# Random-feature attention ahead of two expert layers: projections in plain floats on half arrays, products of heads in column groups

## The chip, the cores and the metric

The program runs on one core of a Trainium2 chip. The metric is device microseconds of that core from one launch, the median of several runs. The engines are named as the profile names them: PE (matmuls; PEld is its weight loads), ACT, DVE, POOL, and SP, which issues the DMAs.

## The reference

Three layers follow each other. The change touches the first.

```python
def phi(x):                                   # x: q or k, scaled by 64 ** -0.25
    proj = np.einsum('bhsd,md->bhsm', x, omega)
    h = proj - np.sum(x * x, axis=-1, keepdims=True) / 2.0
    h = h - np.max(h, axis=-1, keepdims=True)
    return np.exp(h) / np.sqrt(m)
kv = np.einsum('bhsm,bhsd->bhmd', phi(k), v)
z = np.sum(phi(k), axis=2)
num = np.einsum('bhsm,bhmd->bhsd', phi(q), kv)
den = np.einsum('bhsm,bhm->bhs', phi(q), z)[..., None] + 1e-06
x = num / den                                 # 4 batches, 8 heads, 576 positions, 64 wide, 128 features
...
for e in range(8):                            # P: gates, balanced over 8 rounds
    out += P[:, e:e+1] * (np.maximum(x @ w1[e], 0.0) @ w2[e])
...
h = x @ w_in
return (h * (1.0 / (1.0 + np.exp(-1.702 * h)))) @ w_out
```

All inputs are float32.

## The kernel before, in words

**Order.** Every instruction is first recorded with a planned duration and with the buffers that it reads and writes (`Plan.add`, L62). `Plan.run` (L112) then lists the instructions of all engines with those durations: PE's recorded order stays, the rest goes by the latest time at which somebody needs it. Each engine's queue gets its instructions in that order and runs them in order. So a planned duration that changes (the first argument of `pe`, `act`, `dve`) changes the order on every queue, and instructions that nobody edits move too.

**Attention** (L796) goes through 36 tiles of 128 positions by all 8 heads: for each batch its key tiles, then its query tiles. The last 64 positions of two batches share a tile, the tail. Step s of the loop handles tile s and prepares later ones:

- `load_tile` (L505), 8 steps ahead: q, k, v from DRAM into buffers `b2`, of which there are 20. `squares` (L537), 5 ahead: POOL squares a tile, DVE sums it.
- `project_in` (L555), 4 ahead: PE transposes two heads at a time, ACT copies the result, scaled, as rounded floats (`hi`, L567), and DVE writes what the rounding left (`lo`, L570).
- `features` (L577), 2 ahead: PE multiplies by omega, two heads at once: the 128 rows are two heads of 64, and omega stands in a matrix of 128 x 256 whose other blocks are zero. Each pair takes three matmuls, hi by hi, hi by lo, lo by hi (L588 to L590), twelve a tile. DVE takes the minimum over features (L596).
- `exps` (L604): two small sums on DVE, then eight exponentials on ACT, one a head (L626).
- Key tiles: `kv_step` (L635) multiplies features by values and a column of ones into the PSUM tile `pair`, one head after the other (L641). Query tiles: `transpose_q` (L661) turns the features (PE L670, ACT copy L675), `attend` (L682) multiplies them by the sums (L692), `divide` (L704) divides, `transpose_x` (L728) turns the result (PE L735, ACT L739, DVE L742). The query tails alone multiply in two halves of 64 columns, since the two halves belong to two batches.

All these PSUM results but `pair` go round the six banks 0 to 5 (`ps`, L445).

**Behind it.** Six query tiles make a block of tokens; there are three. `x_operands(j)` (L959) mixes a block's tiles into operands for a fast matrix product (POOL for the first two blocks, ACT casts, L990) and sends them to DRAM. The expert layers then run in visits of a pair of weight chunks by a block: `up_fast` (L1208) with seven products of six matmuls for each of two chunks (L1220), whose results DVE mixes (L1252), ACT casts (L1230) and POOL completes (operands `h`, L407), and `down` (L1351; matmuls L1365). Down products on chunk 0 come ahead of chunk 1's last up product, those on chunk 1 right behind it. The weights of the first expert are prepared during attention: loaded into `raw`, summed (`raw_sum`, L1113) and split (`split`, L1119: ACT casts, L1126, POOL subtracts, into `w1x` and `w2x`), in the order w1 chunk 0, w1 chunk 1, w2 chunk 0, w2 chunk 1, all through the one buffer `raw0`, all on POOL. The first products of the first visit stand among attention's last two steps.

```python
def fn(half):                                 # kv_step, L639
    for h in range(4 * half, 4 * half + 4):
        nc.tensor.matmul(
            PAIR[:, h // 4, (h % 4) * VW : (h % 4) * VW + D + 1], f[r, h, :], vv[r, h, 0 : D + 1],
            start=first and h % 4 == 0, stop=last, skip_group_check=True,
        )
```

## Time and profile before

| | |
|---|---|
| runs | 2039.96, 2043.42, 2046.22 us, median 2043.42 |
| profiled execution, its time / its span | 2040.57 / 2038.8 us |
| busy of the span | PE 1984.5 us (97%), DVE 1466.4, POOL 1257.5, ACT 1080.3 |
| attention | 0 to about 188 us, 9% of the span |
| behind it, 500 to 1000 us | PE busy 495.0 of 500 |
| granted TensorE clock, mean | 0.995 |

Busy time is that of instructions, not of arithmetic: a busy PE is not PE at its peak. Matmuls overlap in the trace, so the distance from one start to the next tells what one takes, and a group's span is read from start to start. Idle time of an engine that nobody waits for costs nothing.

### The profile page before, as it was taken

Reading aid. Unit: us, or ns where it says so; the run is one execution under the profiler, and the core shown is the slowest. Engines: PE = TensorE matmul, PEld = TensorE weight load, DVE = VectorE, ACT = ScalarE, POOL = GpSimd, SP = SyncE. Lnnn points to the kernel's source line nnn. Section 1 sums busy time; section 2 is a strip of 40 time slices with the busy share of each in tenths; the row PEclk is TensorE's granted clock in tenths of the full one; section 3 lists DMA queues with packets and bytes.
Section 4 is the critical chain, followed back from the end, with each engine's and each line's share of the span. In section 5 each row is a group of like instructions: output and inputs, shape, how many; then the busy total and the mean of one; then the engine's idle time right before and its main releaser. Section 6 shows DMA issues by size and latency. Waiting matters only on the chain.

```text
span 2038.8 us, 39158 instructions
## 1 busy us (share of the span) xinstructions
PE 1984.5 (97%) x14211; PEld 1948.2 (96%) x14211; DVE 1466.4 (72%) x3040; ACT 1080.3 (53%) x2537; POOL 1257.5 (62%) x1207
## 2 busy tenths in 40 slices
PE   8999999999999999999999999999999979999999
PEld 8998999999999999999999999999999979999998
DVE  8885468777776777777776777766666786667766
ACT  6877563754445354454445345444534566745654
POOL 3677774757666585766657485665648264747453
PEclk9999999999999999999999999999999999999999
DMA  9647664756666575676566576556546897645653
GB/s 188 163 157 260 229 224 176 283 208 221 256 243 213 214 268 198 232 269 224 199 249 237 195 266 242 214 206 233 202 180 244 252 290 259 257 152 218 227 193 129
DMA packets 246898, 451.97 MB, mean 222 GB/s; under 512 B 73648, under 2 KB 186800, under 8 KB 246704
## 3 DMA queue, kind: packets, MB, share of 16 engines
q1 hardware_dynamic: 246704, 449.47, 62.8%
q8 instruction: 112, 1.84, 0.4%
q14 instruction: 82, 0.67, 0.1%
HBM read 403.26 MB, written 46.14 MB: 220 GB/s over the span
## 4 chain that ended last, share of the span: by engine, by line
PE 81%; DVE 11%; DMA 3%; ACT 3%; issue 1%; POOL 1%; SPq 0%; DVEq 0%; ACTq 0%; POOLq 0%
PE bank L1220 38%; PE bank L1365 37%; DVE h L407 2%; DVE ring L1252 2%; PE pair L641 2%; DVE acc L1398 1%; DVE bank L1241 1%; DVE x2s L1041 1%; ACT h L1230 1%; PE bank L588 1%; DMA sx<-x2s 1%; DMA sx<-acc 1%; PE bank L589 1%; PE pair L692 1%; PE bank L590 1%
## 5 line engine op out<-in xcount | busy, mean ns | idle before, releaser
L1365 PE MATMUL bank<-w2x,h 128*128 128x256 f32 x7560 | 940.1, 281 | 33.4 <-DVE acc L1398 11.8
L1365 PEld LDWEIGHTS bank<-w2x,h 128*128 128x128 f32 x7560 | 917.4, 188 | 48.9 <-DVE acc L1398 16.4
L1220 PE MATMUL bank<-xo,w1x 128*128 128x384 f32 x5040 | 915.9, 336 | 3.7 <-ACT ring L1230 1.6
L1220 PEld LDWEIGHTS bank<-xo,w1x 128*128 128x128 f32 x5040 | 866.7, 188 | 10.2 <-ACT ring L1230 6.3
L407 POOL TENSOR_TENSOR h<-ring,h 128x384 fp32r<-128x384 f32 x382 | 413.4, 1107 | 96.2 <-ACT h L1230 93.7
L1398 DVE SCALAR_TENSOR_TENSOR acc<-bank,sig,acc 128x256 f32<-128x256 f32 x756 | 328.4, 478 | 146.6 <-PE bank L1365 145.7
L407 POOL TENSOR_TENSOR w1x<-raw,w1x 128x768 fp32r<-128x768 f32 (+1 forms) x120 | 181.3, 1520 | 265.2 <-ACT w1x L1126 256.3
L1230 ACT ACTIVATE bank<-bank 128x384 f32<-128x384 f32 x120 | 57.0, 475 | 461.7 <-PE bank L1220 435.8
L1230 ACT ACTIVATE ring<-bank 128x384 f32<-128x384 f32 x480 | 233.2, 491 | 125.6 <-PE bank L1220 116.7
L407 POOL TENSOR_TENSOR raw<-raw 128x256 f32<-128x256 f32 x320 | 240.7, 777 | 83.8 <-DMA raw<-in_moe_w_dram 55.0
L1279 DVE SCALAR_TENSOR_TENSOR h<-bank,h 128x384 fp32r<-128x384 f32 x288 | 159.1, 554 | 161.0 <-ACT ring L1230 146.0
L1230 ACT ACTIVATE h<-ring 128x384 fp32r<-128x384 f32 x480 | 231.1, 527 | 68.3 <-DVE ring L1252 58.1
L407 POOL TENSOR_TENSOR w2x<-raw,w2x 128x768 fp32r<-128x768 f32 (+1 forms) x120 | 180.9, 1515 | 54.9 <-ACT w2x L1126 54.5
L1230 ACT ACTIVATE h<-bank 128x384 fp32r<-128x384 f32 x360 | 175.5, 493 | 71.2 <-DVE bank L1241 45.1
L1252 DVE SCALAR_TENSOR_TENSOR ring<-bank,ring 128x384 f32<-128x384 f32 x384 | 192.6, 547 | 24.8 <-PE bank L1220 23.3
L407 POOL TENSOR_TENSOR ring<-ring 128x384 f32<-128x384 f32 (+1 forms) x106 | 112.2, 1059 | 155.4 <-ACT ring L1230 143.6
L1241 DVE TENSOR_TENSOR bank<-bank,ring 128x384 f32<-128x384 f32 x240 | 133.6, 560 | 32.4 <-PE bank L1220 31.3
L1391 DVE TENSOR_TENSOR acc<-bank,acc 128x256 f32<-128x256 f32 x252 | 95.7, 419 | 64.7 <-PE bank L1365 63.7
L1126 ACT CAST w2x<-raw 128x768 fp32r<-128x768 f32 (+1 forms) x120 | 82.4, 692 | 84.1 <-POOL raw L407 69.1
L407 DVE TENSOR_TENSOR h<-ring,h 128x384 fp32r<-128x384 f32 x98 | 99.6, 1027 | 1.3 <-ACT h L1230 1.0
L1126 ACT CAST w1x<-raw 128x768 fp32r<-128x768 f32 (+1 forms) x120 | 82.4, 693 | 13.5 <-PE bank L1220 11.9
L626 ACT ACTIVATE acc<-bank,acc 128x128 f32<-128x128 f32 x272 | 75.7, 390 | 8.7 <-DVE acc L619 6.5
(134 smaller groups left out, 1457.9 us busy)
## 6 DMA issues: line engine op xcount, KB each, us to landing
xo<-sx SPq DMA_DIRECT2D x420, 768.0 KB, 6.8
raw<-in_moe_w_dram SPq DMA_DIRECT2D x256, 128.0 KB, 4.3
sx<-x2s SPq DMA_DIRECT2D x126, 128.0 KB, 4.1
x2s<-in_moe_w_in_dram SPq DMA_DIRECT2D x16, 512.0 KB, 5.4
x2s<-in_moe_w_out_dram SPq DMA_DIRECT2D x16, 512.0 KB, 9.0
sx<-ring SPq DMA_DIRECT2D x32, 192.0 KB, 1.9
b<-in_k_dram SPq DMA_DIRECT2D x16, 256.0 KB, 4.5
b<-in_v_dram SPq DMA_DIRECT2D x16, 256.0 KB, 4.5
```

What stands on the lines that cost most here:

```text
L407: lambda e: e.tensor_tensor(out=out(), in0=a(), in1=b(), op=op), r, w,
L626: lambda h=h, pv=pv: nc.scalar.activation(f[:, h, :], pv[:, h % 4, :], AF.Exp, bias=nb[:, h : h + 1], scale=-1.0),
L641: nc.tensor.matmul(PAIR[:, h // 4, (h % 4) * VW : (h % 4) * VW + D + 1], f[r, h, :], vv[r, h, 0 : D + 1], start=first and h % 4 == 0, stop ...
L1126: lambda e, a=a, b=b: nc.scalar.copy(T[w, c, 0][:, a:b], r[:, a:b]), raws, [(w, c, g, 0)],
L1220: nc.tensor.matmul(o(b), T["w1", c, a][:, slot, kk], T["xo"][x][:, y, kk], start=start and kk == 0 and n == 0, stop=kk == 1 and n == 2, sk ...
L1230: rec("ACT", act_us(Q), lambda e: nc.scalar.activation(out(), src(), f, **kw), r, w)
L1241: lambda e: e.tensor_tensor(out=out[0](), in0=a[0](), in1=b[0](), op=op), [a[1], b[1]], [out[1]],
L1252: lambda e: e.scalar_tensor_tensor(out=RT(out), in0=o(b), scalar=0.0, in1=RT(c), op0=ALU.max, op1=op),
L1279: lambda e: e.scalar_tensor_tensor(out=g(), in0=src[0](), scalar=0.0, in1=h().bitcast(F32), op0=ALU.max, op1=ALU.subtract),
L1365: nc.tensor.matmul(bank[i][:, u], T["h", c, a, x][:, t * P : (t + 1) * P], T["w2", c, y][:, slot], start=s and m == 0, stop=c == 1 and m = ...
L1391: lambda e, q=q, i=i, u=u: e.tensor_tensor(out=q, in0=bank[i][:, u], in1=q, op=ALU.add),
L1398: lambda e, q=q, i=i, u=u, g=g: e.scalar_tensor_tensor(out=q, in0=bank[i][:, u], scalar=g, in1=q, op0=ALU.mult, op1=ALU.add),
```

## The change

Five things change in attention, and the planned durations with them.

1. `project_in` makes one plain copy `xt` in float32 and no `lo`. omega is kept once, as it is (128 rows: twice 64).
2. `features` multiplies in plain float32, one head at a time on its 64 rows: head pairs alternate between rows 0 to 63, into one bank, and rows 64 to 127, into another. Eight heads, eight matmuls in the code.
3. `kv_step` and `attend` split the 128 columns of every tile into two groups of 64.
4. `features` looks three steps ahead, `project_in` five, `squares` six. Features alternate between banks 0, 1 and 2, 3; all transposes go through banks 4 and 5 by turns. The turned query features have one buffer of their own.
5. Of the buffers `b2`, 13 hold raw tiles, 4 hold `xt` and one the tail of the values.

```diff
-    turn = {"ps": [0, 1, 2, 3, 4, 5], "f4": [0, 1, 2, 3], "small": {}}
+    turn = {"t": [4, 5], "f": [0, 1, 2, 3], "f4": [0, 1, 2, 3], "small": {}}
...
-        hi, kh = slot(NP * P, kind="hl")
-        lo, kl = slot(NP * P, kind="hl")
-        hi, lo = hi.bitcast(F32R), lo.bitcast(F32R)
-        act(0.63, lambda: nc.scalar.activation(hi, pt, AF.Copy, scale=-SCALE), [kp], [kh])
-        dve(
-            0.69,
-            lambda: nc.vector.scalar_tensor_tensor(
-                out=lo, in0=pt, scalar=-SCALE, in1=hi.bitcast(F32), op0=ALU.mult, op1=ALU.subtract
-            ),
-            [kp, kh], [kl],
-        )
-        return (hi, kh), (lo, kl)
+        xt, kt = slot(NP * P, kind="xt")
+        act(0.63, lambda: nc.scalar.activation(xt, pt, AF.Copy, scale=-SCALE), [kp], [kt])
+        return xt, kt
...
-                    nc.tensor.matmul(o, hi[:, u], om_hi, start=True, stop=False)
-                    nc.tensor.matmul(o, hi[:, u], om_lo, start=False, stop=False)
-                    nc.tensor.matmul(o, lo[:, u], om_hi, start=False, stop=True)
-            pe(6 * 0.12, fn, [kh, kl, "om0", "om1"], [kp])
...
+            for i in range(NP):
+                for e in range(2):
+                    r = slice(e * D, (e + 1) * D)
+                    nc.tensor.matmul(
+                        pj[e][0][:, i * M : (i + 1) * M], xt[r, i * P : (i + 1) * P], om[r, :],
+                        start=True, stop=True, skip_group_check=True,
+                    )
+        pe(0.95, fn, [kt, "om"], [k for _, k in pj])
...
+    COLUMNS = [slice(i * P // 2, (i + 1) * P // 2) for i in range(2)]
...
-                nc.tensor.matmul(
-                    PAIR[:, h // 4, (h % 4) * VW : (h % 4) * VW + D + 1], f[r, h, :], vv[r, h, 0 : D + 1],
-                    start=first and h % 4 == 0, stop=last, skip_group_check=True,
-                )
+                for c in COLUMNS:
+                    nc.tensor.matmul(
+                        PAIR[c, h // 4, (h % 4) * VW : (h % 4) * VW + D + 1], f[r, h, c], vv[r, h, 0 : D + 1],
+                        start=first and h % 4 == 0, stop=last, skip_group_check=True,
+                    )
...
-            pe(8 * 0.1115, lambda half=half: fn(half), heads(kf)[4 * half : 4 * half + 4] + [kv], [PAIRS[half]])
+            pe(
+                16 * 0.03 + 0.05, lambda half=half: fn(half),
+                heads(kf)[4 * half : 4 * half + 4] + [kv], [PAIRS[half]],
+            )
...
-        parts = ((slice(0, P), kvs[b]),) if t < NT else tuple(
-            (slice(i * TAIL, (i + 1) * TAIL), kvs[b - 1 + i]) for i in range(2)
-        )
+        parts = [(c, kvs[b if t < NT else b - 1 + i]) for i, c in enumerate(COLUMNS)]
```

The order of PE in one key step, before (a half of `features`, then of `kv_step`; L561 is `project_in`, L588 to L590 the projections, L641 the products):

```order
L561 MATMUL bank_103<-ident,b_90 128x128 x4
L588 MATMUL bank_104<-xo 128x256
L589 MATMUL bank_104<-xo 128x256
L590 MATMUL bank_104<-xo 128x256
L588 MATMUL bank_104<-xo 128x256
L589 MATMUL bank_104<-xo 128x256
L590 MATMUL bank_104<-xo 128x256
L641 MATMUL pair<-b_89,acc_72 128x65 x4
```

and in the changed program (L551 `project_in`, L568 the projections, L624 the products):

```order
L551 MATMUL bank_104<-ident,b_90 128x128 x4
L624 MATMUL pair<-b_87,acc_72 64x65 x16
L568 MATMUL bank_101<-ring,b_94 128x128
L568 MATMUL bank_102<-ring,b_94 128x128
L568 MATMUL bank_101<-ring,b_94 128x128
L568 MATMUL bank_102<-ring,b_94 128x128
L568 MATMUL bank_101<-ring,b_94 128x128
L568 MATMUL bank_102<-ring,b_94 128x128
L568 MATMUL bank_101<-ring,b_94 128x128
L568 MATMUL bank_102<-ring,b_94 128x128
L551 MATMUL bank_103<-ident,b_92 128x128 x4
```

The halves of a tile no longer alternate between projections and products: all of a tile's products stand together, then all of its projections, on two banks by turns.

PE in a query step of the changed program (L654 is `transpose_q`, with the buffers' numbers):

```order
L654 MATMUL bank4_103<-ident_63,acc0_72 128x128 x4
L654 MATMUL bank5_104<-ident_63,acc0_72 128x128 x4
L568 MATMUL bank0_99<-ring_69,b215_95 128x128
L568 MATMUL bank1_100<-ring_69,b215_95 128x128
L568 MATMUL bank0_99<-ring_69,b215_95 128x128
L568 MATMUL bank1_100<-ring_69,b215_95 128x128
L568 MATMUL bank0_99<-ring_69,b215_95 128x128
L568 MATMUL bank1_100<-ring_69,b215_95 128x128
L568 MATMUL bank0_99<-ring_69,b215_95 128x128
L568 MATMUL bank1_100<-ring_69,b215_95 128x128
L551 MATMUL bank4_103<-ident_63,b24_84 128x128 x4
```

All transposes, of queries, of raw tiles and of results, now go through bank 4 and bank 5.

The order of POOL at the first visit, before, from the sums of chunk 1 of the down weights on (`raw0` the sums, `w2x` the splits, `acc1` the third block, names with `h` the operands of the first visit: in `h021` the first digit is the chunk, 0, the second the operand):

```order
L407 TENSOR_TENSOR raw0_67<-raw0_67 128x256 x3
L407 TENSOR_TENSOR w2x_71<-raw0_67,w2x_71 128x768
L407 TENSOR_TENSOR w2x_71<-raw0_67,w2x_71 128x512
L407 TENSOR_TENSOR acc1_73<-x2s_75,acc2_74 128x384
L407 TENSOR_TENSOR w2x_71<-raw0_67,w2x_71 128x512
L407 TENSOR_TENSOR acc1_73<-x2s_75,acc1_73 128x384
L407 TENSOR_TENSOR ring_69<-ring_69 128x384
L407 TENSOR_TENSOR acc1_73<-x2s_75,acc1_73 128x384
L407 TENSOR_TENSOR acc1_73<-acc1_73,acc2_74 128x384 x2
L407 TENSOR_TENSOR acc1_73<-acc1_73,x2s_75 128x384
L407 TENSOR_TENSOR acc1_73<-acc1_73 128x384
L407 TENSOR_TENSOR h021_2087<-ring_69,h020_2086 128x384
```

and now, from the first operand of the visit on:

```order
L402 TENSOR_TENSOR h031_2316<-ring_69,h030_2315 128x384
L402 TENSOR_TENSOR ring_69<-ring_69 128x384
L402 TENSOR_TENSOR raw0_67<-raw0_67 128x256
L402 TENSOR_TENSOR h021_2314<-ring_69,h020_2313 128x384
L402 TENSOR_TENSOR h041_2318<-ring_69,h040_2317 128x384
L402 TENSOR_TENSOR h141_2332<-ring_69,h140_2331 128x384
L402 TENSOR_TENSOR raw0_67<-raw0_67 128x256 x3
L402 TENSOR_TENSOR w2x_71<-raw0_67,w2x_71 128x768
```

The sums and the split of chunk 1 stood ahead of all operands of the visit; they now stand behind h141, an operand of chunk 1 itself.

## Rows read from the trace of the kernel before

**Rows 1.** the page's head.
```profile
span 2038.8 us, 39158 instructions
```

**Rows 2.** timeline of PE, attention's end to the first down products: start us, us, engine, instructions.
```profile
187.40 0.66 PE L735 MATMUL bank<-ident,acc 128*128 128x128 f32 x4 [0.82 <-DVE acc L721]
...
201.04 1.22 PE L1365 MATMUL bank<-w2x,h 128*128 128x256 f32 x9
...
203.14 1.10 PE L1365 MATMUL bank<-w2x,h 128*128 128x256 f32 x8
```

**Rows 3.** windows in us: PE, PEld, DVE, ACT, POOL busy (instructions); clock, DMA share, GB/s.
```profile
20.00:140.00 120.00, 115.22 (x995) 111.18 (x995) 103.89 (x263) 97.28 (x289) 70.25 (x80) 0.99 0.70 173
140.00:188.00 48.00, 45.00 (x398) 43.24 (x397) 28.51 (x72) 37.16 (x105) 32.19 (x34) 1.00 0.53 186
```

**Rows 4.** timeline of PE over a key step; columns as in rows 2.
```profile
20.22 0.61 PE L561 MATMUL bank<-ident,b 128*128 128x128 f32 x4
...
20.58 0.36 PE L588 MATMUL bank<-xo 128*128 128x256 f32 x1
...
21.38 1.00 PE L641 MATMUL pair<-b,acc 128*128 128x65 f32 x8
...
22.19 0.36 PE L588 MATMUL bank<-xo 128*128 128x256 f32 x1
```

**Rows 5.** timeline of PE, half of a query tail.
```profile
96.33 0.69 PE L692 MATMUL pair<-raw,acc 128*64 128x65 f32 x16
96.95 0.66 PE L735 MATMUL bank<-ident,acc 128*128 128x128 f32 x4
```

**Rows 6.** timeline of PE, half of a key tail, on 64 rows.
```profile
32.27 1.10 PE L641 MATMUL pair<-b,ring 64*128 64x65 f32 x8
33.30 0.39 PE L588 MATMUL bank<-xo 128*128 128x256 f32 x1
```

**Rows 7.** groups of DVE by line, 20 to 140 us: count, busy us, mean ns, idle.
```profile
L570 DVE SCALAR_TENSOR_TENSOR xo<-bank,xo 128x512 fp32r<-128x512 f32 x25 | 17.0, 681 | 0.0
```

**Rows 8.** timeline of ACT, a copy of transposes and a tile's exponentials.
```profile
139.74 0.59 ACT L675 COPY acc<-bank 128x512 f32<-128x512 f32 x1
...
142.41 2.18 ACT L626 ACTIVATE acc<-bank,acc 128x128 f32<-128x128 f32 x8
```

**Rows 9.** timeline of PE after a stop; idle us and releaser in brackets.
```profile
103.22 1.08 PE L641 MATMUL pair<-b,acc 128*128 128x65 f32 x8 [2.56 <-POOL acc L541]
...
104.58 1.27 PE L641 MATMUL pair<-b,acc 128*128 128x65 f32 x8
...
108.97 0.36 PE L588 MATMUL bank<-xo 128*128 128x256 f32 x1
```

**Rows 10.** timeline of POOL, the second block's first mixes and chunk 1's splits.
```profile
147.67 1.97 POOL L407 TENSOR_TENSOR ring<-w2x,xo 128x384 f32<-128x384 f32 x2
...
188.46 3.11 POOL L407 TENSOR_TENSOR w2x<-raw,w2x 128x768 fp32r<-128x768 f32 x2
```

**Rows 11.** groups of POOL by line and shape, 147 to 205 us.
```profile
L407 POOL TENSOR_TENSOR ring<-ring,xo 128x384 f32<-128x384 f32 x8 | 7.9, 1004 | 0.1
...
L407 POOL TENSOR_TENSOR ring<-ring 128x384 fp32r<-128x384 f32 x8 | 7.9, 1003 | 3.5 <-ACT ring L990 3.4
...
L407 POOL TENSOR_TENSOR raw<-raw 128x256 f32<-128x256 f32 x4 | 2.8, 731 | 7.7 <-DMA raw<-in_moe_w_dram 7.7
```

**Rows 12.** the page, part 5, groups by line over the span.
```profile
L407 POOL TENSOR_TENSOR h<-ring,h 128x384 fp32r<-128x384 f32 x382 | 413.4, 1107 | 96.2 <-ACT h L1230 93.7
...
L1230 ACT ACTIVATE h<-ring 128x384 fp32r<-128x384 f32 x480 | 231.1, 527 | 68.3 <-DVE ring L1252 58.1
...
L407 POOL TENSOR_TENSOR w2x<-raw,w2x 128x768 fp32r<-128x768 f32 (+1 forms) x120 | 180.9, 1515 | 54.9 <-ACT w2x L1126 54.5
...
L1252 DVE SCALAR_TENSOR_TENSOR ring<-bank,ring 128x384 f32<-128x384 f32 x384 | 192.6, 547 | 24.8 <-PE bank L1220 23.3
```

**Rows 13.** window as in rows 3, behind that stop.
```profile
105.00:108.00 3.00, 3.00 (x18) 3.00 (x17) 1.58 (x4) 2.95 (x10) 3.00 (x4) 0.53 0.66 244
```

More of the change, by code (lines that the diff above doesn't have):

```diff
@@ L343, in tile_performer_sinkhorn_moe @@
     att = opened(att_pool, "att")
[L344 to L345 removed]
+    for i in range(18):
+        slots["b2" if i < 13 else "xt" if i < 17 else "vt"].append((att.tile([P, H * VW], F32, name=f"b2{i}"), ("b2", i)))
+    F4.append(att.tile([P, H, M], F32, name="f4"))
     H_KEYS = [("h", c, o, a) for c in range(2) for o in range(7) for a in range(2)]
@@ L443, in heads, with ps @@
         return [(key, h) for h in range(H)]
-    def ps():
-        i = taken("ps")
+    def ps(what="t"):
+        i = taken(what)
         return bank[i], ("b", i)
@@ L510, in load_tile @@
         w = VW if what == "v" else D
-        x, kx = raw[key] = slot(H * w, H)
+        x, kx = raw[key] = slot(H * w, H, kind="vt" if key[2] == "tail" and what == "v" else "b2")
         if what == "v":
@@ new lines, in project_in, with features, fn @@
+        act(0.63, lambda: nc.scalar.activation(xt, pt, AF.Copy, scale=-SCALE), [kp], [kt])
+        return xt, kt
+    def features(xt, four):
+        (xt, kt), (four, kf) = xt, four
+        pj = [ps("f") for _ in range(2)]
+        def fn():
+            for i in range(NP):
[6 more added lines that the diff above has]
+        pe(0.95, fn, [kt, "om"], [k for _, k in pj])
+        pvs = [(p.rearrange("p (h m) -> p h m", m=M), k) for p, k in pj]
+        for e, (pv, kp) in enumerate(pvs):
@@ L594, in features @@
             dve(
                 0.69,
-                lambda half=half, pv=pv: nc.vector.tensor_reduce(
-                    out=four[:, H + 4 * half : H + 4 * half + 4], in_=pv, op=ALU.min, axis=AX.X
+                lambda e=e, pv=pv: nc.vector.tensor_reduce(
+                    out=four[:, H : 2 * H].rearrange("p (i e) -> p e i", e=2)[:, e], in_=pv, op=ALU.min, axis=AX.X
                 ),
@@ L809, in column @@
             return divmod(PLACE[token_tile(*seq[i][1:])], ST)
[L811 removed]
+        for s in range(-6, n + 3):
             what, b, t = seq[s] if at(s, "kq") else (None, 0, 0)
             if s == n - 2:
[L814 to L843 removed]
+                plan.add("X", 0.0, lambda e: switch(), (), [k for _, k in slots["b2"] + slots["xt"] + slots["vt"]] + heads(("f4", 4)) + H_KEYS)
+            if at(s + 6, "kq"):
+                squares(*seq[s + 6])
+            if s == -6:
+                products_of_zeros(10)
+            if what == "q":
+                ft = transpose_q(feat.pop(s))
+            if s == -1:
+                products_of_zeros(10)
+            if at(s + 3, "kq"):
+                four = sums.pop(seq[s + 3])
+                pvs = features(ins.pop(s + 3), four)
+                w, b2, t2 = seq[s + 3]
                 if w == "k" and t2 == NT:
@@ L848, in attention @@
                     f2 = F4[i], ("f4", i)
-                feat[s + 2] = f2
-            if what == "q":
-                next(tq)
-                yield s - n, 0
-                steps = [attend(ft, b, t)]
-            if steps:
-                next(steps[0])
-            if at(s + 2, "kq"):
+                feat[s + 3] = f2
                 exps(pvs, four, f2)
+            if at(s + 5, "kq"):
+                ins[s + 5] = project_in(*seq[s + 5])
             if at(s - 1, "q"):
                 transpose_x(xs.pop(s - 1), *column(s - 1))
-            for x in steps:
-                take(x, 3)
+            if what == "q":
+                yield s - n, 0
+                attend(ft, b, t)
+            elif what == "k":
+                f = feat.pop(s)
+                last = seq[s + 1][0] == "q"
+                kv_step(b, t, f, t == 0, last and b % 2 == 0)
+                if last and b % 2 == 1:
+                    kv_step(b, NT, ktail.pop(b // 2), False, True)
             yield s - n, 1
```

75 lines of the change are left out of this document (10 added, 65 removed).

## The prediction

> **What bounds the kernel now.** I read the windows first, then the timelines of PE and POOL, then the groups by line. The span is 2038.8 us [rows 1]; the profiled execution took 2040.57 us as a whole, and the median of the three runs, 2043.42 us, stands 2.85 us above it. The change touches attention alone, which ends with PE's last transposes at 187.40 us [rows 2]. From 20 to 140 us PE is busy 115.2 of 120, that is 96%; DVE 103.9, ACT 97.3, POOL 70.3 [rows 3]. So PE sets the pace there, but three engines lie close together: cutting PE's work is worth no more than the way down to the next engine. From 140 to 188 us PE has 45.0 of 48, ACT 37.2 [rows 3].
>
> A key step of PE begins at 20.22 us: transposes to 20.58, six projections to 21.38, four heads' products to 22.19 [rows 4]; then the other six projections and the other four heads. So a tile's twelve projections take 2 x 0.80 = 1.60 us and its eight heads' products 2 x 0.81 = 1.62 us. Each head's product stands as two matmuls in the trace (x8 for four heads), so one takes 0.81 / 8 = 0.101 us.
>
> **The products in two column groups.** One kind of tile works so already, the tails of the queries: a half of sixteen matmuls of 64 columns lies between 96.33 and 96.95 us, 0.62 us with the change of form behind it [rows 5]. The other tiles go from 1.62 to at most 2 x 0.62 = 1.24 us: **0.38 us saved** for each of 36 tiles less the two query tails. A half of a key tail lasted from 32.27 to 33.30 us [rows 6], so a tail, of which there are four, 2.06 us; it comes to 1.24 too, 0.8 us saved.
>
> A matmul of 64 columns thus took 0.62 / 16 = 0.039 us, below the 0.05 that half of 0.101 would be without any overlap. The Trainium skill ("TensorE: Matmul & The Clock Gate", Part 3: Packing small matmuls) holds that weights load beside a running matmul only where the row group differs, which speaks against column groups. By that rule I estimate 0.05 x 16 = 0.8 us a half and no saving on products: PE would keep 100.9 us of the first window where I find 89.8 below, and attention would gain 22.6 us, not 23.4. The measurement decides.
>
> **The projections on 64 rows.** Eight heads are sixteen matmuls of 128 columns, alternately from two halves of the array and into two banks, as the new order of PE shows. No row has two row halves at work at once. Bounds: 0.039 us each, as for column groups, or 0.101 us each if the halves take turns; and the change of form, which on the key tail cost 1.03 - 0.81 = 0.22 us [rows 4, 6]. That makes 0.84 to 1.84 us, against 1.60. I take half of 0.101, since two halves share the work but each still streams all 128 columns, which no column group did: 0.81 + 0.22 = 1.03 us, **0.57 us saved** a tile. The low operand goes too: DVE loses 25 subtractions in the first window, 17.0 us of its 103.9 [rows 7].
>
> **What attention becomes.** In the first window 25 projections, some 23 products and three key tails fall: 25 x 0.57 + 23 x 0.38 + 3 x 0.8 = 25.4, PE 115.2 - 25.4 = 89.8 us. DVE has 103.9 - 17.0 = 86.9. ACT keeps its 97.3 and is now first. With three engines within 11 us of each other, and two banks for transposes where six went round, I give ACT not the 96% that PE had but 93%: 97.3 / 0.93 = 104.6 us, **15.4 us gained**. At 96% it would be 18.6; at 87%, midway to the 81% that ACT has now, 8.2. In the second window PE falls by 11 x 0.57 + 10 x 0.38 + 0.8 to 34.1, and ACT's 37.2 / 0.93 = 40.0: **8.0 us gained** (9.2 and 5.2 at the ends). Together 23.4 us, so the last transposes come at 187.4 - 23.4 = 164.0 us.
>
> The Trainium skill ("TensorEngine Tiling (Array Packing)", PSUM Bottleneck) warns that tiling makes the matmuls faster but not the copies out of PSUM, which then may set the pace. PE alone would give 25.4 + 10.9 = 36.3 us; the windows side with the warning, as ACT's share stands above what PE has left.
>
> Small edits: one copy of omega in place of two masked halves, a prologue longer by a step, 13 buffers of raw tiles where 20 were. I take nothing for them. The prologue moves exponentials ahead, eight in 2.18 us [rows 8], which later steps have behind them; loads still stand eight steps ahead, and DMA had a share of 0.70 [rows 3]. If that cover goes, the price is a stop such as the one before 103.22 us, 2.56 us [rows 9].
>
> **What is late next.** POOL's work is not cut, and stands in another order. The first expert's weights are split by POOL alone, chunk after chunk through one buffer, with the mixes of the second block of tokens (x_operands) among them. Before, POOL took up that block at 147.67 us and reached chunk 1 of the down weights at 188.46 [rows 10]; PE wanted them at 203.14 [rows 2], so nobody waited. Now chunk 1 of w1 comes behind most of the block, then both chunks of w2. From the block's first mix to the first split of w2's chunk 0 POOL has 32 mixes of 1.00 us, 10 sums of 0.73 and 5 splits of 1.52 [rows 11, 12]: 32.1 + 7.3 + 7.6 = 47.0 us, and 3.5 us of waits for ACT as now [rows 11]. The block can begin 15.4 + 8.0 x 7.67 / 48 = 16.7 us earlier, at 131.0; chunk 0 is then there at 181.5. PE reaches the first down products 201.04 - 187.40 = 13.6 us behind the last transposes [rows 2], at 177.6: it **waits 3.9 us**.
>
> Chunk 1 is worse. Its split now stands on POOL behind h141, the rest of an operand that needs PE's last up product, and PE's down products on chunk 1 come right behind that product. So PE stops for a whole chain: three mixes on DVE, 3 x 0.55; a cast on ACT, 0.53; h141, 1.11; three sums, 3 x 0.73; the split, 1.52 [rows 11, 12]: **7.0 us**. The kernel before has no such wait.
>
> Then the clock. After the stop of 2.56 us the granted clock was 0.53 from 105 to 108 us, so mostly the lower level, 1.2 GHz [rows 9, 13]; from 104.58 to 108.97 us PE took 4.39 us for what takes 0.81 + 0.36 + 0.80 + 0.81 = 2.78 at 2.4 GHz [rows 4, 9]. I add **1.6 us** once.
>
> **The sum.** -23.4 + 3.9 + 7.0 + 1.6 = -10.9 us. On the profiled execution that is 2040.57 - 10.9 = 2029.7 us; runs lie up to 2.85 us above such an execution, and I add half of it: **2031.1 us**.
>
> **Rivals.**
> *POOL keeps up.* The sums and the split of chunk 1 are done before PE comes, and the chain lies beside other products. For it: POOL is busy only 70.3 of 120 us [rows 3]. Against it: the order is fixed. All of 23.4 us stays: 2040.57 - 23.4 + 1.4 = 2018.6 us. Chance 0.22.
> *ACT and DVE get in each other's way.* At 87% attention gains 13.4 us. The second block begins 9.1 us earlier, and POOL's chunk 0 is there at 147.67 - 9.1 + 50.5 = 189.1, PE at 187.4 - 13.4 + 13.6 = 187.6: 1.5 us of waiting, then 7.0 and 1.6. That is -3.3 us, 2038.7 us, and within 0.3% of no change (6.1 us, about what a measurement of this kernel can tell). Chance 0.23.
> *The two banks stop PE: slower.* All transposes, four groups in a query step, now go through banks 4 and 5 by turns. A turn holds a bank for 0.36 us of PE, 0.59 of ACT's copy and whatever stands ahead of the copy on ACT [rows 4, 8]. A query step of PE takes about 1.60 + 1.62 + 4 x 0.36 = 4.66 us before; with two turns a bank in each step, the banks set it once a turn is over 2.33 us, when a copy waits over 1.4 us, five of eight exponentials [rows 8]. If it waits for all eight, a turn is 3.13 us and a step 6.26: 18 x 1.6 = 29 us lost, against 18 x 0.65 = 11.7 gained in key steps, with 8.6 of chain and clock: 2068 us. Against it: in ACT's new order most copies stand between exponentials. Chance 0.10.
> *The row halves take turns.* Projections at 1.84 us: PE has 115.2 + 25 x 0.24 - 23 x 0.38 - 2.4 = 110.1 us, at 96% 114.6, so 5.4 us gained, and 3.2 in the second window; POOL is in time then, chain and clock cost 8.6: 2042.0 us. Chance 0.07.
>
> **How the numbers follow.** The sum above has the rest, 0.38, and lies between 2024 and 2037 by itself. From 2017 to 2044 all cases are held but the slow one and the outer ends of others. Faster by over 0.3%, below 2037.3 us: 0.37 of the forecast, 0.21 of the first rival and 0.05 of the second, 0.63. Within 0.3%: 0.26. Slower: 0.11.
>
> **What would show it.** Right: sixteen projections in about 1 us; a half of products in about 0.6; attention's last transposes near 164 us; PE idle some 7 us before the down products on chunk 1, released by POOL's split, and a lower granted clock behind it. Wrong: transposes that wait for ACT's copies in every query step; projections 0.1 us apart; no gap at the first down products; an attention that ends after 175 us.

## The result and the profile after

The changed kernel takes **2025.82 us** (median of 4 runs, 2024.18 to 2028.46); the kernel before, on the same chip, 2044.82 us (4 runs, 2039.96 to 2048.07). The ratio is 0.991, with a 95% interval from 0.9886 to 0.9935: faster by 0.9%. The forecast was 2031.1 us in a range from 2017 to 2044, and faster with a chance of 0.63. The two medians lie 19.0 us apart; beside the later experiments the kernel before had medians of 2041.2 to 2041.6 us and the changed one, run again (e12 below), 2026.07, so some 3.5 us of the 19.0 come from a kernel before that was slower in that measurement than in the later ones.

The page of the changed kernel, against [rows 1]:

```profile
span 2026.7 us, 40550 instructions
PE 1961.8 (97%) x14931; PEld 1910.6 (94%) x14931; DVE 1430.7 (71%) x2994; ACT 1078.1 (53%) x2536; POOL 1263.8 (62%) x1213
```

The span is 12.1 us shorter. Its windows, of which the first answers to [rows 3] (columns: stretch and length; busy us of PE, PEld, DVE, ACT, POOL; granted clock; DMA share; GB/s):

```profile
20.00:140.00 120.00, 109.48 (x1746) 93.48 (x1748) 102.36 (x266) 107.24 (x334) 69.57 (x83) 0.99 0.72 189
140.00:168.00 28.00, 23.67 (x319) 20.38 (x316) 10.69 (x28) 19.65 (x52) 22.52 (x23) 0.94 0.73 248
168.00:188.00 20.00, 15.70 (x94) 13.29 (x92) 9.71 (x20) 12.62 (x28) 18.52 (x20) 1.00 0.86 292
188.00:212.00 24.00, 17.79 (x129) 17.50 (x130) 4.90 (x10) 9.78 (x25) 23.64 (x26) 0.86 0.44 165
```

In the first window PE (91%), ACT (89%) and DVE (85%) stand within 8 us of each other. Behind it POOL fills up: from 188 us it is busy for 23.64 of 24 us, while PE stands still for a quarter of them.

PE's timeline of a key step, against [rows 4] (start, us, engine, line and operation; products L624, projections L568, transposes L551), and of a key tail, against [rows 6]:

```profile
23.39 1.15 PE L624 MATMUL pair<-b,acc 128*64 128x65 f32 x32
24.47 1.16 PE L568 MATMUL bank<-ring,b 64*128 64x128 f32 x16
25.57 0.65 PE L551 MATMUL bank<-ident,b 128*128 128x128 f32 x4
26.15 1.16 PE L624 MATMUL pair<-b,acc 128*64 128x65 f32 x32
...
31.68 1.15 PE L624 MATMUL pair<-b,ring 64*64 64x65 f32 x32
32.76 1.27 PE L654 MATMUL bank<-ident,acc 128*128 128x128 f32 x8
```

From start to start a tile's products take 1.08 us (1.62 before), its projections 1.10 (1.60), a tail's products 1.08 (2.06).

The end of attention and the first visit of the experts, against [rows 2] (L716 are attention's transposes, L1331 the down products, nine on chunk 0 and then 108 on chunk 1):

```profile
167.65 0.60 PE L716 MATMUL bank<-ident,acc 128*128 128x128 f32 x4
...
178.98 5.50 PE L1186 MATMUL bank<-xo,w1x 128*128 128x384 f32 x30 [2.58 <-ACT bank L1196]
184.32 1.22 PE L1331 MATMUL bank<-w2x,h 128*128 128x256 f32 x9
185.37 1.21 PE L1186 MATMUL bank<-xo,w1x 128*128 128x384 f32 x6
192.53 0.58 PE L1331 MATMUL bank<-w2x,h 128*128 128x256 f32 x1 [5.95 <-ACT w2x L1092]
194.79 14.29 PE L1331 MATMUL bank<-w2x,h 128*128 128x256 f32 x107 [1.68 <-POOL w2x L402]
208.91 1.21 PE L1186 MATMUL bank<-xo,w1x 128*128 128x384 f32 x6
209.96 1.22 PE L1331 MATMUL bank<-w2x,h 128*128 128x256 f32 x9
```

Attention ends 19.75 us earlier than before (187.40). Up to the first down products PE then takes 16.67 us, where it took 13.64, with a stop of 2.58 us. In front of chunk 1 it stops for 5.95 and again for 1.68 us. The 0.86 of the granted clock in the last window is a mean over stretches at 1.2 and at 2.4 GHz. The second block's first down products, at 209.96 us, stood at 216.78 in the kernel before: of 19.75 us 6.82 are left there.

What POOL did in the stop (raw sums, L402 `raw`; the operands' rests, `h`; splits, `w2x`):

```profile
178.05 4.30 POOL L402 TENSOR_TENSOR w2x<-raw,w2x 128x768 fp32r<-128x768 f32 x3
...
186.72 0.72 POOL L402 TENSOR_TENSOR raw<-raw 128x256 f32<-128x256 f32 x1 [0.46 <-DMA raw<-in_moe_w_dram]
187.40 3.53 POOL L402 TENSOR_TENSOR h<-ring,h 128x384 fp32r<-128x384 f32 x3
190.89 2.08 POOL L402 TENSOR_TENSOR raw<-raw 128x256 f32<-128x256 f32 x3
192.93 3.04 POOL L402 TENSOR_TENSOR w2x<-raw,w2x 128x768 fp32r<-128x768 f32 x2
```

Chunk 0 is split until 182.35 us; only then may chunk 1 be loaded into the same raw buffer, and it lands at 186.7. Three rests of h stand ahead of the last three sums, and the split begins at 192.93: the chain of the forecast, with a load ahead of the sums that the forecast did not have, and three rests of h where it had one.

### The profile page after: what moved, and what is told of

It is laid out like the page before. It is cut to its first block, busy times and chain, and to the rows that moved or that the text cites. A ratio compares the mean times of both kernels' runs of the same rounds, so it can differ in the third digit from the quotient of the medians.

```text
span 2026.7 us, 40550 instructions
## 1 busy us (share of the span) xinstructions
PE 1961.8 (97%) x14931; PEld 1910.6 (94%) x14931; DVE 1430.7 (71%) x2994; ACT 1078.1 (53%) x2536; POOL 1263.8 (62%) x1213
## 4 chain that ended last, share of the span: by engine, by line
PE 81%; DVE 10%; ACT 3%; DMA 3%; POOL 2%; issue 1%; SPq 0%; DVEq 0%; ACTq 0%; POOLq 0%
PE bank L1186 39%; PE bank L1331 38%; DVE h L402 2%; DVE ring L1218 1%; DVE acc L1364 1%; DMA sx<-x2s 1%; PE bank L568 1%; DVE bank L1207 1%; DVE acc L578 1%; ACT acc L607 1%; DVE acc L538 1%; ACT h L1196 1%; POOL ring L402 1%; DMA xo<-sx 1%; DVE x2s L1007 1%
## 5 line engine op out<-in xcount | busy, mean ns | idle before, releaser
L1331 PE MATMUL bank<-w2x,h 128*128 128x256 f32 x7560 | 943.4, 282 | 35.0 <-DVE acc L1364 9.1
L1331 PEld LDWEIGHTS bank<-w2x,h 128*128 128x128 f32 x7560 | 920.2, 189 | 51.2 <-DVE acc L1364 13.5
L402 POOL TENSOR_TENSOR h<-ring,h 128x384 fp32r<-128x384 f32 x384 | 416.2, 1109 | 94.0 <-ACT h L1196 91.8
L402 POOL TENSOR_TENSOR w1x<-raw,w1x 128x768 fp32r<-128x768 f32 (+1 forms) x120 | 181.6, 1523 | 268.2 <-ACT w1x L1092 259.8
L402 POOL TENSOR_TENSOR raw<-raw 128x256 f32<-128x256 f32 x320 | 238.8, 772 | 76.0 <-DMA raw<-in_moe_w_dram 49.4
L402 POOL TENSOR_TENSOR ring<-ring 128x384 f32<-128x384 f32 (+1 forms) x108 | 113.1, 1049 | 157.0 <-ACT ring L1196 149.8
L402 POOL TENSOR_TENSOR w2x<-raw,w2x 128x768 fp32r<-128x768 f32 (+1 forms) x120 | 182.8, 1532 | 43.7 <-ACT w2x L1092 39.4
L1092 ACT CAST w2x<-raw 128x768 fp32r<-128x768 f32 (+1 forms) x120 | 82.3, 692 | 91.2 <-POOL raw L402 76.2
L402 DVE TENSOR_TENSOR h<-ring,h 128x384 fp32r<-128x384 f32 x96 | 97.9, 1032 | 2.0 <-ACT h L1196 1.7
L1092 ACT CAST w1x<-raw 128x768 fp32r<-128x768 f32 (+1 forms) x120 | 83.3, 698 | 17.7 <-PE bank L1186 16.1
```

The lines of the kernel that those rows point to most:

```text
L402: lambda e: e.tensor_tensor(out=out(), in0=a(), in1=b(), op=op), r, w,
L1092: lambda e, a=a, b=b: nc.scalar.copy(T[w, c, 0][:, a:b], r[:, a:b]), raws, [(w, c, g, 0)],
L1331: nc.tensor.matmul(bank[i][:, u], T["h", c, a, x][:, t * P : (t + 1) * P], T["w2", c, y][:, slot], start=s and m == 0, stop=c == 1 and m = ...
```

## The experiments

Each ratio is against runs of the kernel before that were taken beside it (median 2044.82 us beside the changed kernel, 2041.2 to 2041.6 us beside the experiments). "Ninth" and "last" are the starts of the 9th and 18th groups of the transposes of attention's results (L716), "down" the start of the first down products, "chunk 1" that of the first unbroken run of down products on chunk 1 (a single one ahead of it is left out).

| kernel | ninth | last | down | chunk 1 | median us | ratio, 95% interval |
|---|---|---|---|---|---|---|
| before | 104.14 | 187.40 | 201.04 | 203.14 | 2044.82 | 1 |
| changed | 90.19 | 167.65 | 184.32 | 194.79 | 2025.82 | 0.991 (0.9886 to 0.9935) |
| e12, changed again | 89.54 | 161.65 | 180.61 | 190.40 | 2026.07 | 0.9916 (0.9892 to 0.994) |
| e2, whole columns | 98.27 | 173.93 | 187.58 | 189.68 | 2025.06 | 0.9926 (0.9902 to 0.995) |
| e8, hi and lo | 102.00 | 174.56 | 188.22 | 190.31 | 2027.02 | 0.9929 (0.9914 to 0.9944) |
| e11, neither | 108.14 | 192.28 | 205.91 | 208.00 | 2044.06 | 1.0011 (0.9997 to 1.0024) |
| e3, halves in turn | 100.84 | 175.96 | 195.33 | 205.11 | 2035.68 | 0.9967 (0.9955 to 0.998) |
| e1, second raw buffer | 89.53 | 166.95 | 181.36 | 183.46 | 2020.24 | 0.9897 (0.9878 to 0.9915) |
| e4, two exponentials | 86.45 | 161.64 | 178.10 | 188.53 | 2022.92 | 0.9912 (0.9892 to 0.9932) |
| e7, two ahead | 88.24 | 160.20 | 178.81 | 188.55 | 2024.27 | 0.9912 (0.9897 to 0.9927) |
| e5, six banks | 102.13 | 179.10 | 192.70 | 194.80 | 2028.64 | 0.9932 (0.9916 to 0.9948) |
| e6, e1 and products on POOL | 87.63 | 162.82 | 178.85 | 181.23 | **2017.52** | 0.988 (0.9864 to 0.9896) |
| e9, e6 and two ahead | 87.88 | 159.05 | 183.06 | 188.60 | 2018.88 | 0.9887 (0.9861 to 0.9913) |
| e10, e9 and sums shared | 88.06 | 158.48 | 179.99 | 183.53 | 2018.51 | 0.9882 (0.986 to 0.9903) |

### How far one trace can be read: e12

No edit. Expected:

> The changed kernel once more, for a second trace of it. Between the profiles of before and of the change 5.3 of the 12.1 us lie behind the first expert, where no line was changed. If these come from the planner's other order of the later work, the second trace repeats them: from 209.96 us to the end again 1816.7 us within 1 us, with the same waits. Rival: they are scatter between runs; then this stretch differs by 2 us or more.

From the second block's first down products (205.72 us here) to the end at 2024.5 it took 1818.8 us, where the first trace had 1816.7 and the kernel before 1822.0. The two traces of one kernel differ by 2.1 us; over the traces of the other eleven kernels it is 1813.6 to 1822.9. So of the 5.3 us behind the first visit none can be told from scatter, and none is shown to come from the planner's order.

The second trace says more. The ninth transposes agree within 0.65 us, but the last came at 161.65, 6.0 us earlier. Here is one step in which the traces part, DVE and POOL in the first trace:

```profile
118.08 2.29 DVE L538 TENSOR_SCALAR acc<-acc 128x8 f32<-128x8 f32 x2
120.28 0.68 DVE L578 TENSOR_REDUCE acc<-bank 128x4 f32<-128x512 f32 x1
...
121.28 0.68 DVE L723 TENSOR_TENSOR xo<-bank,w2x 128x512 fp32r<-128x512 f32 x1
```

POOL in the same trace:

```profile
117.29 3.04 POOL L402 TENSOR_TENSOR w1x<-raw,w1x 128x768 fp32r<-128x768 f32 x2
```

and DVE and POOL in the second trace:

```profile
116.62 0.23 DVE L538 TENSOR_SCALAR acc<-acc 128x8 f32<-128x8 f32 x2
...
117.72 3.04 POOL L402 TENSOR_TENSOR w1x<-raw,w1x 128x768 fp32r<-128x768 f32 x2
```

Two products of 128x8 took 0.23 us or 2.29, as they came ahead of POOL's splits or among them; the late pair ended with the splits (120.37 and 120.33 us). PE then stood for 2.61 us for the transposes' bank, which L723 had to empty, and the granted clock was 0.76 from 120 to 126 us. A later part of the 6.0 us, about 1.4, goes with a granted clock of 0.50 from 164.1 to 167.5 us, in a stretch of attention that the second trace has at 1.00. So an end of attention from a single trace counts below only where it differs by more than 6 us; the ninth transposes, before that point, are taken as good to 1 us. Two traces give no better measure of the scatter than this.

### The two main parts, alone and not at all: e2, e8, e11

e2, products in one matmul of 128 columns each (`attend` likewise):

```diff
-                for c in COLUMNS:
+                for c in (slice(0, P),):
...
-    parts = [(c, kvs[b if t < NT else b - 1 + i]) for i, c in enumerate(COLUMNS)]
+    parts = [(slice(0, P), kvs[b])] if t < NT else [(c, kvs[b - 1 + i]) for i, c in enumerate(COLUMNS)]
```

> The changed kernel with the products of heads back in one matmul of 128 columns each (1.62 us a tile for 1.08). If the column groups paid as PE time, 36 tiles take 0.54 us more each, 19 us, less the 10.5 us of PE's idle time in the window 20 to 140 us that it can fill: attention's last transposes come 8 to 15 us later than 167.65 us, and as POOL is then in time the whole is 2 to 8 us slower than the changed kernel. Rival: ACT paces attention now, and the column groups are worth nothing: last transposes within 3 us of 167.65, total within 2 us.

e8, the projections as they were:

```diff
-        act(0.63, lambda: nc.scalar.activation(xt, pt, AF.Copy, scale=-SCALE), [kp], [kt])
...
+        act(0.63, lambda: nc.scalar.activation(hi, pt, AF.Copy, scale=-SCALE), [kp], [kh])
+        dve(
+            0.69,
+            lambda: nc.vector.scalar_tensor_tensor(
+                out=lo, in0=pt, scalar=-SCALE, in1=hi.bitcast(F32), op0=ALU.mult, op1=ALU.subtract
+            ),
+            [kp, kh], [kl],
+        )
...
+                    nc.tensor.matmul(o, hi[:, u], om_hi, start=True, stop=False)
+                    nc.tensor.matmul(o, hi[:, u], om_lo, start=False, stop=False)
+                    nc.tensor.matmul(o, lo[:, u], om_hi, start=False, stop=True)
```

> The changed kernel with the projections as they were: twelve matmuls of 128 rows from a rounded operand and the rest that DVE subtracts; column groups, banks and the third step stay. PE takes 1.60 us for 1.09 a tile, 0.51 x 36 = 18 us more, and DVE gets 36 subtractions of 0.68 us back, 24 us, some 17 to 20 of them in the window 20 to 140 us where it has 102.4 of 120 us. I expect DVE to become the first: attention's last transposes at 182 to 190 us, near the kernel before (187.40), and a total of 2035 to 2044 us. Rival: the column groups carry the gain by themselves, since PE set the pace before: last transposes at 172 to 180 us.

e11 has both edits:

> The changed kernel without both of its main parts: products in 128 columns and projections from a rounded operand and the rest. What is left of the change is the third step ahead, the banks set apart, the buffers and the planner's costs, for which I took nothing. If they are worth nothing, attention's last transposes come within 3 us of the kernel before, 184 to 190 us, and the whole is 2036 to 2044 us. Rival: they are worth some 6 to 7 us, since each main part alone left 13 to 13.5 us of the 19.75: last transposes near 180 us. A third: they cost, as the third step did in e7: over 190 us.

At the ninth transposes the column groups are worth 98.27 - 89.54 = 8.7 us (8.1 against the first trace) and the projections 12.5 (11.8); together, by e11, 18.6 (18.0), where the two worths sum to 21.2. They nearly add up, and the two parts are the whole gain. The other edits alone (e11) do not help: 4.0 us later at the ninth transposes, the last at 192.28 (the third case of the expectation), and no difference in the whole that the interval tells from none. PE stopped more in e11's window from 20 to 140 us, and the granted clock was 0.94 there against 0.99.

In the whole, either part alone reaches what both together reach; I had expected e2 to be 2 to 8 us slower and e8 to take 2035 to 2044 us, and both missed. The first visit of e2 shows why:

```profile
173.93 0.66 PE L716 MATMUL bank<-ident,acc 128*128 128x128 f32 x4
187.58 1.22 PE L1331 MATMUL bank<-w2x,h 128*128 128x256 f32 x9
189.68 12.76 PE L1331 MATMUL bank<-w2x,h 128*128 128x256 f32 x108
```

Attention ends 6.3 us later than in the changed kernel's first trace, but POOL has chunk 1 ready, PE does not stop, and the products on it begin at 189.68 for 194.79. With both parts the second one's gain in attention is paid back at the first expert. The end of attention that I expected for e8 (182 to 190 us) missed too: DVE had 111.50 of 120 us, yet attention ended at 174.56, so DVE at 93% still kept up.

### Two row halves at once: e3

```diff
-            for i in range(NP):
-                for e in range(2):
+            for e in range(2):
+                for i in range(NP):
```

> The changed kernel with the sixteen projections of a tile in another order: the eight on rows 0 to 63 first, then the eight on rows 64 to 127, each to the same place as before. If the time of 1.09 us comes from two row halves at work at once, halves in turn take about 0.1 us a matmul, 1.6 to 1.8 us a tile, 36 x 0.6 = 22 us more of PE, and attention ends 10 to 20 us later. Rival: a matmul on 64 rows is itself quicker than one on 128, and the order does not matter: still about 1.1 us, and the same total within 2 us.

A tile's projections, at the full clock:

```profile
36.95 1.71 PE L568 MATMUL bank<-ring,b 64*128 64x128 f32 x16
38.59 0.66 PE L551 MATMUL bank<-ident,b 128*128 128x128 f32 x4
```

1.64 us where alternating halves take 1.10: 0.103 us a matmul, as the trace counts them, against 0.069. The instructions are the same, so the order alone is worth 0.54 us a tile. The whole is 9.9 us slower, and attention's ninth transposes come 10.7 us later, part of it from a granted clock of 0.56 between 26 and 36 us. The forecast's half of 0.101 plus 0.22 for the change of form came out at 1.03 for 1.10.

The single records show the two halves at once. In the first trace of the changed kernel a tile's sixteen projections start in pairs, 0.007 us between the two of a pair and 0.112 us from pair to pair; the matmuls of 128 columns of `kv_step` before started 0.112 us apart, one at a time. In e3 only three pairs stand in the middle of the sixteen, and most other starts stand alone, 0.112 us apart: taken in the code's order, the second half begins 0.55 us behind the first and runs beside its end. So 1.64 us is not yet fully in turn; sixteen starts 0.112 us apart would be 1.8 us, by an estimate from these rows.

### The stop in front of chunk 1: e1

```diff
-                    prepare(0, "w2", 1, 0)
-                    split("w2", 1, 0)
+                    prepare(0, "w2", 1, 1)
+                    split("w2", 1, 1)
```

> The changed kernel with one difference: chunk 1 of the first expert's down weights goes through the second raw buffer, so that it need not wait for chunk 0's split, and its sums and splits move ahead of the rest of h141 on POOL. If, as I hold, POOL's order makes the stop before the down products on chunk 1 (8.2 us from 186.58 to 194.79 us, and 22.3 us from 186.58 to the next expert products at 208.91 where the kernel before took 12.6), the stop falls to under 3 us and the kernel is 5 to 9 us faster than the changed kernel: about 2017 to 2021 us. Rival: POOL as a whole is full from 157 us on, whatever its order; then the stop stays over 5 us, or moves to the first down products, and the gain is under 2 us.

```profile
166.95 0.60 PE L716 MATMUL bank<-ident,acc 128*128 128x128 f32 x4
181.36 1.22 PE L1331 MATMUL bank<-w2x,h 128*128 128x256 f32 x9
182.42 1.20 PE L1186 MATMUL bank<-xo,w1x 128*128 128x384 f32 x6
183.46 6.82 PE L1331 MATMUL bank<-w2x,h 128*128 128x256 f32 x57
190.73 6.28 PE L1331 MATMUL bank<-w2x,h 128*128 128x256 f32 x51 [0.46 <-ACT acc L1353]
```

With attention ending as late as in the first trace of the changed kernel, the stop is gone, chunk 1 begins 11.3 us earlier, and the whole is 5.6 us faster: 2019.77 to 2020.90 us, against 2021.03 to 2028.46 in the eight runs of the changed kernel. The stop was the raw buffer and POOL's order, not POOL's amount of work: from 20 to 195 us POOL is busy for 117.61 us in the changed kernel and 118.31 in e1.

The edit changes both at once, the load that waits for chunk 0's split and, through the plan, POOL's order, and no run tells them apart. An estimate from POOL's rows above: with nothing of POOL's between the load, the sums and the split, the four sums of 2.80 us and the 1.86 us from the split's start to PE's, counted from 186.72, would have let PE go on at 191.4 us instead of 194.79, so about 3.4 of the 8.2 us hang on the order and the rest on the load.

### Who paces attention now: e4, e7, e5, e6

e4 takes work from ACT:

```diff
-        for h in range(H):
+        for h in range(2):
...
-                    f[:, h, :], pv[:, h // 2, :], AF.Exp, bias=nb[:, h : h + 1], scale=-1.0
+                    f[:, 4 * h : 4 * h + 4, :], pv[:, 0:4, :], AF.Exp, bias=nb[:, h : h + 1], scale=-1.0
```

> The changed kernel with less work for ACT: a tile's eight exponentials of 128 columns, each with its own head's offset, become two of 512 columns with one offset each, so the offsets of six heads are left out. ACT loses about 2.2 - 1.1 = 1.1 us a tile, 36 to 40 us in all. If ACT paces attention at 89 to 93 percent, as my forecast holds, PE then sets the pace: the waits of PE for exponentials and copies go, and attention's last transposes come 6 to 12 us earlier than 167.65 us. Rival: DVE (102.4 of 120 us busy) and the two transpose banks that wait for it pace attention; then the waits of PE for DVE stay (11 us of idle time) and the end moves by less than 3 us. The total moves little in either case, as POOL is late already: 0 to 4 us.

The window from 20 to 140 us, columns as in [rows 3], of e12 (no edit) and of e4:

```profile
20.00:140.00 120.00, 112.18 (x1833) 96.29 (x1833) 100.77 (x265) 110.19 (x344) 70.75 (x83) 1.00 0.75 198
20.00:140.00 120.00, 113.59 (x1865) 97.23 (x1864) 103.75 (x270) 85.72 (x158) 75.65 (x88) 1.00 0.76 205
```

ACT fell to 85.72 of the 120 us, from 107.24 and 110.19 in the two traces of the changed kernel; PE rose to 113.59, 95%, from 109.48 and 112.18. The ninth transposes came 3.1 to 3.7 us earlier; the last at 161.64, as in e12, so the 6 to 12 us that I expected there are not shown. A fifth of ACT's load off is worth some 4% of the 90 us up to the ninth transposes. ACT is one of the pacers, not the first.

e7 goes back to two steps ahead:

```diff
-            if at(s + 3, "kq"):
-                four = sums.pop(seq[s + 3])
-                pvs = features(ins.pop(s + 3), four)
+            if at(s + 2, "kq"):
+                four = sums.pop(seq[s + 2])
+                pvs = features(ins.pop(s + 2), four)
```

> The changed kernel with features, transposes and squares one step less ahead, as in the kernel before: features two steps ahead in place of three, the prologue a step shorter. I took nothing for this edit. If so, attention's last transposes stay within 2 us of 167.65 us. Rival: with ACT near 90 percent busy the eight exponentials are late at PE without the third step: PE's products wait for them in most steps, and attention ends 4 to 12 us later.

Ninth transposes 1.3 to 2.0 us earlier, the last at 160.20 (7.5 us ahead of the first trace, 1.5 of e12's), the whole 1.6 us below with overlapping runs (2021.03 to 2025.94). The third step buys nothing that can be seen.

e5 gives transposes and features one rotation of six banks:

```diff
-    turn = {"t": [4, 5], "f": [0, 1, 2, 3], "f4": [0, 1, 2, 3], "small": {}}
+    six = [0, 1, 2, 3, 4, 5]
+    turn = {"t": six, "f": six, "f4": [0, 1, 2, 3], "small": {}}
```

> The changed kernel with one rotation of six banks for transposes and features, as in the kernel before, in place of two for transposes and four for features. In the changed kernel PE waited 5.5 us in the window 20 to 140 us for transposes whose bank DVE had not yet emptied. If the two banks cost that, these waits fall under 1.5 us and attention's last transposes come 3 to 6 us before 167.65 us. Rival: the banks only show the pace of DVE and ACT, and six let a transpose take a bank that features need: the waits turn up in front of the projections, and the end stays within 2 us or is later.

This kernel does not compute quite the same output as the others, and why stays open; so it is no variant to use, and only its times are read. Its matmuls are the same in kind and number. PE's longest waits from 20 to 190 us (line and what it waited for; us in total, times, longest):

```profile
PE bank L569 <- ACT acc L608: 13.4, 12, 2.1
PE bank L717 <- DVE acc L703: 2.7, 3, 1.0
```

The rival held: the transposes of the query features no longer wait for a bank that DVE has to empty (5.5 us in the changed kernel's first trace), but projections (L569 here) wait 13.4 us for exponentials that hold their banks. The ninth transposes came 12 us later. As far as these times show, the banks set apart serve the change.

e6, on top of e1, moves the two products of 128x8 from DVE to POOL:

```diff
-            dve(
+            pool(
                 0.16,
-                lambda a=a, y=y: nc.vector.tensor_scalar(
+                lambda a=a, y=y: nc.gpsimd.tensor_scalar(
```

> The kernel with the second raw buffer (e1), and the two products of 128x8 per tile that DVE makes in the squares on POOL instead. On DVE they took 21.9 us of the window 20 to 140 us, 0.40 us each where the shortest took 0.12, and the long ones ended with an instruction of POOL. If DVE's pace matters, DVE falls from 101 to about 82 of the 120 us, PE's waits for DVE (5 to 8 us) go and attention's last transposes come 3 to 7 us before the 166.95 us of e1; the whole is 2 to 6 us under 2020.2 us. Rival: ACT alone paces attention, and POOL, with 60 more small operations of some 0.15 us, is later with its splits: end of attention within 2 us, whole 0 to 4 us slower.

On POOL each takes 0.23 us, without spread:

```profile
L538 POOL TENSOR_SCALAR acc<-acc x59: 231/232/238, 19.9 to 123.8; 128x8 f32<-128x8 f32 x59
```

DVE has 89.40 of 120 us for 101.42, attention's ninth transposes come 1.9 us earlier, and the whole is 2.7 us below e1: 2016.64 to 2017.81 us. That is the lower edge of what was expected, and the best kernel of the study: 8.3 us below the changed one and 1.2% (1.0 to 1.4) below the one before.

### Is there more in attention's end: e9, e10

e9 is e6 with e7's two steps; e10 also lets DVE take raw sums of the first expert (`"VP", **kw` in `prepare`).

> Three edits to the changed kernel at once: the second raw buffer (e1), the 128x8 products on POOL (e6) and two steps ahead in place of three (e7). Alone they gave 5.6 us, 2.7 us and 1.6 us of the whole. If attention's end and the stops behind it add up, attention ends at 155 to 160 us and the whole is 2008 to 2015 us. Rival: POOL's work on the first expert's weights and the second block's mixes sets the end from 150 us on, so that an earlier attention only waits longer: first down products no earlier than 176 us, whole 2015 to 2020 us.

> As e9, and the sums of the first expert's raw tiles may go to DVE as well as to POOL, as those of the later experts do. If POOL's work sets the end of the stage, DVE takes some 10 sums of 0.73 us from it and the first down products come 2 to 7 us before those of e9, the whole 2 to 5 us faster. Rival: PE has all it wants in e9; then no difference over 2 us, or a loss where DVE's sums stand ahead of its work on banks.

```profile
159.05 0.66 PE L716 MATMUL bank<-ident,acc 128*128 128x128 f32 x4
183.06 0.58 PE L1331 MATMUL bank<-w2x,h 128*128 128x256 f32 x1 [8.93 <-ACT w2x L1092]
184.95 2.07 PE L1331 MATMUL bank<-w2x,h 128*128 128x256 f32 x8 [1.31 <-POOL w2x L402]
```

The gains do not add up: e9 takes 2018.88 us, inside the range of its rival, and e10 differs from it by 0.4 us with overlapping runs. In e9 attention ends 3.8 us before e6, which is within the scatter, and the first down products come 4.2 us after: the stop has moved in front of chunk 0. In e10 they come at 179.99, and PE waits for chunk 1 of w1 instead (2.7 us for ACT's cast, 2.6 for POOL's split). From 150 to 180 us DMA's share is 0.97 in e9 and 0.82 in e10, POOL's busy time 24.5 and 23.1 of 30 us. Whether POOL, DMA or the order of the two sets this floor was not told apart. Over all kernels whose attention ended from 158 to 168 us, the first down products came between 178 and 185 us.

## Why the forecast was right, and where it was off

**The terms for PE** held. Projections 1.10 us for 1.03, products 1.08 for 1.24, tails 1.08 for 1.24; the first two errors have opposite signs, and a tile saves 0.50 + 0.54 = 1.04 us where 0.57 + 0.38 = 0.95 was forecast. Products start in pairs too, one pair every 0.059 us, so in both terms two matmuls are under way at once. From a rule on weight loads in the Trainium skill ("TensorE: Matmul & The Clock Gate", Part 3: Packing small matmuls) I estimated no saving on products; the same section also gives a measured gain for column tiles, which that estimate left aside. The runs decide against the estimate: e2 shows 8.1 to 8.7 us saved at the ninth transposes.

**"ACT is now first, at 93%"** failed in part. ACT rose to 107.24 us, 89% of the window, and to 92% in the second trace, but PE stayed above it with 91% and 93%, and e4 shows that a fifth less of ACT's work gives back only 3.1 to 3.7 us up to the ninth transposes. The warning of the Trainium skill ("TensorEngine Tiling (Array Packing)", PSUM Bottleneck) is borne out only so far. What paces the steps, as far as the waits show it, is that three engines near 90% wait for each other in turn, and now and then a chain through DVE and POOL; no single run proves it. The size was right all the same: last transposes at 164.0 us were forecast, and the two traces have 167.65 and 161.65.

**The first down products** were to wait 3.9 us. Against 13.64 us behind attention's end they came 3.0 us late in the first trace, and 5.3 in the second (18.96 us). The place was another: PE stopped in front of an up product, released by ACT, where the three casts of chunk 0 (L1092, 2.01 us from 175.77) stood ahead of the copies that PE needed; POOL's splits, until 182.35 us, were in time for PE at 184.32.

**The stop in front of chunk 1** and the clock were to cost 7.0 + 1.6 = 8.6 us. From the first down products to those of the second block it took 25.64 us where it took 15.74: 9.9 us, and 9.4 in the second trace (25.11 us). The stop alone is 5.95 + 1.68 = 7.6 us, and 6.9 in the second trace. The clock cost what was set down for it: behind the stop 107 products take 14.12 us, where e2, without the stop and at the full clock, needs 12.60 for 108, so about 1.6 us more. The chain that I listed is there, with one link that I left out: chunk 1's load, which waits for chunk 0's split. By the estimate under e1 this link carries the larger part of the stop, so the 7.0 us came out nearly right from a chain that was not the whole one, and that is in part luck. e1, which cuts the link and changes POOL's order with it, takes the stop away.

**The sum** up to the second block was -10.9 us; the traces have -6.8 and -11.1. The rest was outside of the forecast: I took all that lies behind the first visit as unchanged, and it was 5.3 and 3.2 us shorter in these traces than in the one of before. e12 shows that this stretch scatters by 2 us and more with one kernel, so part of the agreement of the whole is luck, and where the rest comes from stays open. So too the 1.4 us for runs above the profiled one: the first trace's own run, 2028.46 us, was the slowest of its four.

**The rivals.** POOL did not keep up. DVE and ACT in each other's way turned up in a third form, DVE behind POOL, in single steps. The two banks stopped PE for 5.5 us of attention in the first trace and 2.1 in e12, far from the 29 that would have made it slower, and e5's six are worse. Row halves do not take turns, as long as the order alternates; made to for the most part, they cost 9.9 us of the whole. In the sum of the second rival the block begins 9.0 us earlier, not 9.1, which moves its time by 0.1 us.

**The small edits** at nothing: right for the sum (e11, 1.0011). For the third step ahead nothing speaks in the runs.

## What to carry to other kernels

Matmuls on 64 rows each paid here only with the two halves alternating in PE's order: look at the order, not only at the shapes. When an early stage gets quicker, ask next who prepares the data of the stage behind it, through which buffer and in which order: here a second raw buffer, two numbers in two lines, was worth 5.6 us of the whole, while the column groups, on top of the projections, shortened attention and not the whole. Compare two traces of the same kernel before explaining a difference of a few microseconds, and measure at a mark that they agree on.

## What the runs showed of the hardware

A DVE product of 128x8 took 0.12 us at least and 1.31 us at most in the window from 20 to 140 us, and all 18 that took over 0.5 us ended 0.03 us behind the end of an instruction of POOL; those under 0.25 us ran with POOL idle or began within 0.2 us of the start or the end of an instruction of POOL. The kernel before has the same form (1.30 us at most, nine over 0.5 us, all ending so), so it is not the change's.

```profile
L538 DVE TENSOR_SCALAR acc<-acc x60: 119/165/1305, 20.0 to 130.8; 128x8 f32<-128x8 f32 x60
```

In the changed kernel these sixty instructions (the three times are least, median and most, in ns) had 21.9 us, where sixty of the median 0.165 us are 9.9. The Trainium skill ("GPSIMD Engine Reference", Key points) says that POOL shares its SBUF interfaces with DVE and contends with some forms of DVE instruction; the trace agrees, with up to 1.31 us for an instruction that takes 0.165 in the median.

As the trace counts them, a float32 matmul of 64 columns takes 1.08 / 32 = 0.034 us where one of 128 takes 0.101, a third and not a half; one of 128 columns on 64 rows takes 0.069 with alternating halves and 0.103 with one half after the other. Two column groups, and two row halves that alternate, run at once: starts come in pairs, 0.007 us within a pair, and from pair to pair 0.059 us for the column groups and 0.112 us for the row halves.
